# Attention, then two MLPs on one core: where 1 / sum is multiplied in, and when the weight product is made

## The chip, the cores and the metric

The kernel runs on one core of a Trainium2 chip. The metric is the device time of one execution in microseconds. The core has a tensor engine (TensorE, PE in the profile; PEld is its weight load), VectorE (DVE), ScalarE (ACT), GpSimd (POOL) and SyncE (SP), which here only issues transfers. Each engine works through its own list of instructions in order; semaphores make one wait for another.

## The reference

Attention with RMS-normed q and k over 4 batches of 12 heads, 448 positions and 64 features, and then two MLPs over the 1792 tokens of 768 features:

```python
def rmsnorm(x, g):
    return x / np.sqrt(np.mean(x * x, axis=-1, keepdims=True) + 1e-06) * g
scores = 1.0 / np.sqrt(D) * np.matmul(rmsnorm(q, g_q), rmsnorm(k, g_k).transpose(0, 1, 3, 2))
attn = np.exp(scores - np.max(scores, axis=-1, keepdims=True))
attn = attn / (np.sum(attn, axis=-1, keepdims=True) + 1e-09)
x = np.matmul(attn, v).transpose(0, 2, 1, 3).reshape(B * S, H * D)
h = x @ w_in                                  # 768 x 2048
x = np.maximum(0.01 * h, h) @ w_out           # 2048 x 768
return ((x @ w1) * (x @ w2) @ w3) @ w_out2    # 768 x 1024, 1024 x 1024, 1024 x 768
```

The MLP weights arrive as 64-bit floats.

## The kernel before, in words

The heads are worked off in 24 pairs `t`, each in two halves; a half is a *slot*, and slot `2t + half` holds the scores of pair `t`, chunks `2 half` and `2 half + 1` of 112 query rows. `attention_steps` writes the work of a slot in this order: at an even slot the value product of pair `t - 2` (`values`), then the four transposes of p for head `s - 2` (`p_transpose`), then `scores`; after an odd slot come the keys of the next pair (`keys`: transposes into `pk`, split into `kh` and `kl`), the load of q and the squares for the norm three pairs ahead (`statistics`); after an even slot the loads of v and of the rows of q and k three pairs ahead. `run_later` issues at the end of a slot the transfers that were put off.

`scores` multiplies in three passes (high and low parts of q and k, 12 matmuls a slot, tile `ps`), VectorE takes the scaled minimum out of PSUM into `p` (L254), ScalarE makes the exponent in place and sums it along the row (L263). Then VectorE makes `r = 1 / (sum + 1e-9)` for the half (L268, L269), and GpSimd multiplies each of the four `p` tiles by it, row by row (L272), before the tensor engine transposes them (L286). The value product `po` holds the two heads of a pair, 64 features each, over 128 partitions, with the 448 positions along the free axis. For batches 0 and 1 `split` makes of it the high part `xh` (ScalarE) and the low part `xl` (VectorE), both out of PSUM; for batches 2 and 3 ScalarE copies it to `x`, and SP stores that to `xd` in DRAM.

Between the attention's steps a generator of other work is drawn on, at a pace that `fill` sets from the slots that it is given. First `combine_weights` makes `wc = w3 x w_last` (tile `pw`, 384 matmuls); it stands in slots 5 to 17, by `COMBINE_SLOTS`. From there to slot 26 the first MLP of batch 0 runs for two of its four groups (the *early* part, tile `ps_mm`), then the *late* part with batch 1 and the rest; batches 2 and 3 follow as the *last pair* when the heads are done. The weights come as 64-bit words over ScalarE's queue (the first four over SP's); GpSimd, ScalarE and VectorE turn each tile into a float32 (`raw`, on VectorE L427 and L431) and split it into `wh` and `wl` (or `lasth` and `lastl` for w_last, on VectorE L184). The weights of the early part are kept in DRAM as high and low parts for the late one (`kept_first_mlp_h`, `_l`), which GpSimd's queue stores and SP's loads.

In which order the instructions of an engine stand is decided when the program is built, by a list scheduler that takes what is ready in its own model of time, by priority; `issue_after` ties an instruction behind another on its engine.

Of the kernel before, what the change touches and what calls it, by code (L numbers as in the profile page):

```python
# [8 lines left out]
F32 = mybir.dt.float32  # L9
# [3 lines left out]
ALU = mybir.AluOpType  # L13
# [23 lines left out]
KEYS_AHEAD = 1  # L37
P_TILES = 8
TOGETHER = 2000
COMBINE_SLOTS = 5, 17  # L40
EARLY = 2
PRIORITY = dict(
    values=200, p_transpose=600, scores=600, prep=600, load=100, statistics=100, keys=50
# [4 lines left out]
def attention_then_moe(  # L48
# [40 lines left out]
    def bank(name):  # L89
        return psum.tile([P, 512], F32, tag="ps", name=name)  # L90
# [45 lines left out]
    def statistics(t):  # L136

        if t >= NH // 2:
            return
        x = pairs[t]["rows"]  # L140
        ss = small.tile([CP, 2, 2, NCH], F32, tag="ss", name="ss", bufs=2)
        after = exps.get(t - STATS_AHEAD)
        for part in (1, 0):
            y = x[:, part]
            if part:
                y = io.tile([CP, 2, NCH, D], F32, tag="sq", name="sq", bufs=1)
            with tc.issue_after(after.ins) if after else ExitStack():
                nc.scalar.activation(y, x[:, part], AF.Square)
            nc.vector.tensor_reduce(ss[:, part], y, axis=AX.X, op=ALU.add)
        nc.vector.tensor_scalar(ss, ss, 1.0 / D, 1e-6, op0=ALU.mult, op1=ALU.add)  # L150
        rs = small.tile([CP, 2, 2, NCH], F32, tag="rs", name="rs", bufs=4)
        y = small.tile([CP, 2, 2, NCH], F32, tag="y", name="y", bufs=2)
        nc.scalar.activation(y, ss, AF.Ln)
        nc.scalar.activation(rs, y, AF.Exp, scale=-0.5)
        nc.vector.scalar_tensor_tensor(y, rs, -0.5, rs, op0=ALU.mult, op1=ALU.mult)  # L155
        nc.vector.tensor_tensor(y, y, ss, op=ALU.mult)
        nc.vector.scalar_tensor_tensor(rs, y, 1.5, rs, op0=ALU.add, op1=ALU.mult)
        nc.vector.tensor_scalar_mul(rs[:, 0], rs[:, 0], -1.0 / D**0.5)
        pairs[t]["scale"], pairs[t]["rk"] = rs[:, 0], rs[:, 1]
# [65 lines left out]
    def scores(t, half):  # L225

        if t >= NH // 2:
            return
        x = pairs[t]
        pair = heads[2 * t : 2 * t + 2]  # L230
        if half == 0:
            x["sums"] = small.tile([CP, 2, NCH], F32, tag="sum", name="sum")
            for h in pair:
                h["p"] = [None] * NCH
        ps = [[bank("ps")[:CP, :S] for _ in range(2)] for _ in range(2)]
        chunks = range(2 * half, 2 * half + 2)
        terms = [("qh", "kh"), ("ql", "kh"), ("qh", "kl")]
        x["scored"] = together(
            (
                ps[c % 2][e],  # L240
                x[q][mine(e), c * CP : (c + 1) * CP],
                x[k][mine(e)],
                n == 0,
                n == len(terms) - 1,
            )
            for c in chunks
            for n, (q, k) in enumerate(terms)
            for e in range(2)
        )
        for c in chunks:  # L250
            for e, h in enumerate(pair):
                p = h["p"][c] = att.tile([CP, S], F32, tag="p", name="p", bufs=P_TILES)
                low = small.tile([CP, 1], F32, tag="low", name="low", bufs=8)
                nc.vector.tensor_scalar(  # L254
                    p,
                    ps[c % 2][e],
                    x["scale"][:, e, c : c + 1],
                    None,
                    op0=ALU.mult,
                    op1=ALU.min,  # L260
                    accum_out=low,
                )
                exps[t] = nc.scalar.activation(  # L263
                    p, p, AF.Exp, bias=low, scale=-1.0, accum_out=x["sums"][:, e, c : c + 1]
                )

        r = small.tile([CP, 2, 2], F32, tag="r", name="r")
        nc.vector.tensor_scalar_add(r, x["sums"][:, :, 2 * half : 2 * half + 2], 1e-9)  # L268
        nc.vector.reciprocal(r, r)  # L269
        for c in chunks:  # L270
            for e, h in enumerate(pair):
                nc.gpsimd.tensor_scalar(  # L272
                    h["p"][c], h["p"][c], r[:, e, c % 2 : c % 2 + 1], 1.0, op0=ALU.mult, op1=ALU.mult
                )

    def mine(i):
        return slice(D * (i % 2), D * (i % 2 + 1))
# [20 lines left out]
    def split(x, hi, lo, eng="P"):  # L298

        copy("A", hi, x)  # L300
        subtract(eng, lo, x, hi)
# [6 lines left out]
    def values(t):  # L308
# [5 lines left out]
        if j == 0 and b < PB:  # L314
# [4 lines left out]
            for kc in reversed(range(NCH))  # L319
            for e in (1, 0)  # L320
        )
        if b < PB:
            split(po[:, :S], *(y[:, j // 2] for y in xt[b]), "V")
        else:
            x = att.tile([P, S], F32, tag="x", name="x", bufs=1)
            copy("A", x, po[:, :S])
            later.append(lambda: nc.sync.dma_start(xd[b - PB, j // 2], x))
        for h in (*pair, pairs[t]):
            h.clear()
# [8 lines left out]
    def ranked(f, *args):  # L338
        with tc.high_priority(PRIORITY.get(f.__name__, 0)):
            f(*args)  # L340

    def attention_steps():

        for t in range(NH // 2 + 2):
            ranked(values, t - 2)
            yield 2 * t
            for half in range(2):
                s = 2 * t + half
                for kc in range(NCH):
                    ranked(p_transpose, s - 2, kc)  # L350
                    yield s
                ranked(scores, t, half)
                for _ in range(NCH):
                    yield s
                if half:
# [721 lines left out]
```

## Time and profile before

| what | us |
|---|---|
| median of 3 runs (lowest, highest) | 1235.17 (1234.72, 1236.8) |
| the profiled execution | 1229.4 |
| its span, first to last instruction | 1227.6 |
| PE busy in it | 1157.6 (94%) |
| DVE busy | 777.9 (63%) |
| ACT busy | 662.7 (54%) |
| POOL busy | 390.2 (32%) |

Busy times are sums over the whole span; the stages in it have different limits, and an engine's idle time costs nothing where another sets the pace. The mean granted TensorE clock was 0.967 of full speed.

### The profile page before, as it was taken

The page shows a single profiled execution, that of the slowest core. Times are in us where ns is not written, and L with a number is a line of the kernel's source. Part 1 is how long each engine was busy: PE and PEld are TensorE (multiplying, and loading weights), DVE is VectorE, ACT ScalarE, POOL GpSimd, SP SyncE. Part 2 cuts the span into 40 slices and gives each one's busy share as a digit, 9 for nine tenths or more (in the row PEclk, how much of TensorE's full clock was granted, in tenths as well). Part 3 has the DMA queues.
Part 4 walks back from the last instruction along what each step waited for, and adds up shares of the span by engine and source line. Part 5 has one row for each costly group of instructions (what it writes and reads, how often), then busy time and mean ns, then how long its engine had stood idle before and what let it go on. Part 6 is the DMA issues. An engine that isn't in the chain of part 4 may idle for free.

```text
span 1227.6 us, 17006 instructions
## 1 busy us (share of the span) xinstructions
PE 1157.6 (94%) x6096; PEld 966.4 (79%) x6096; DVE 777.9 (63%) x1511; ACT 662.7 (54%) x1343; POOL 390.2 (32%) x474
## 2 busy tenths in 40 slices
PE   2779999998979999999999999999999999899998
PEld 1456778776668788888878888888999999699997
DVE  7997777889852375857854465276346455954553
ACT  7676667777644475666654664245443334533431
POOL 3654345677731344367642443200000000000000
PEclk8669999998889999999999999999999999999999
DMA  8433335877576534534421441062212021112202
GB/s 256 143 99 108 113 123 199 303 257 262 186 298 193 172 119 157 165 126 165 166 88 64 152 161 53 34 227 64 77 35 78 26 77 59 58 39 67 72 35 99
DMA packets 65381, 158.93 MB, mean 129 GB/s; under 512 B 7440, under 2 KB 32784, under 8 KB 65296
## 3 DMA queue, kind: packets, MB, share of 16 engines
q1 hardware_dynamic: 45648, 73.94, 19.0%
q10 hardware_dynamic: 10944, 49.29, 12.0%
q0 software_dynamic: 8704, 34.61, 7.5%
q8 instruction: 48, 0.79, 0.3%
q14 instruction: 37, 0.30, 0.1%
HBM read 114.95 MB, written 42.86 MB: 129 GB/s over the span
## 4 chain that ended last, share of the span: by engine, by line
PE 64%; DVE 7%; DMA 4%; ACT 1%; issue 1%; POOL 1%; SPq 0%; ACTq 0%; DVEq 0%; POOLq 0%
PE ps_mm L499 26%; PE ps_o L499 13%; PE ps_b L499 9%; PE ps_c L499 5%; PE po L123 3%; PE pt L286 3%; PE ps L123 3%; PE ps_a L499 2%; DVE ol L184 1%; DVE wl L184 1%; DMA wh<-kept_first_mlp_h 1%; DMA qk_sb<-qk 1%; DMA x_f<-xd 1%; DMA w<-w_out 1%; DVE acc L863 1%
## 5 line engine op out<-in xcount | busy, mean ns | idle before, releaser
L272 POOL TENSOR_SCALAR p<-p,r 112x448 f32<-112x448 f32 x192 | 150.9, 802 | 63.4 <-DVE r L269 34.4
L184 DVE TENSOR_TENSOR wl<-raw,wh 128x512 fp32r<-128x512 f32 (+1 forms) x136 | 113.9, 839 | 74.9 <-ACT wh L705 35.1
L499 PE MATMUL ps_mm<-xh,wh 128*128 128x448 f32 x384 | 143.0, 373 | 7.3 <-DMA wh<-kept_first_mlp_h 7.0
L263 ACT ACTIVATE p<-p,low 112x448 f32<-112x448 f32 x192 | 126.5, 661 | 40.4 <-DVE p L254 40.1
L499 PE MATMUL ps_mm<-xl,wh 128*128 128x448 f32 x384 | 146.8, 382 | 0.0
L499 PE MATMUL ps_mm<-xh,wl 128*128 128x448 f32 x384 | 141.9, 370 | 0.1
L254 DVE TENSOR_SCALAR_CACHE_REDUCE p<-ps,rs 112x448 f32<-112x448 f32 x192 | 122.0, 678 | 27.7 <-PE ps L123 27.7
L286 PE MATMUL pt<-ident,p 112*112 112x112 f32 x768 | 107.2, 278 | 25.7 <-POOL p L272 20.7
L286 PEld LDWEIGHTS pt<-ident,p 112*112 112x112 f32 x768 | 87.5, 143 | 52.8 <-POOL p L272 26.6
L499 PE MATMUL ps_mm<-gl,wh 128*128 128x448 f32 x288 | 109.5, 380 | 0.0
L427 DVE SCALAR_TENSOR_TENSOR raw<-w,raw 128x768 uint32<-128x768 uint32 (+1 forms) x80 | 76.0, 949 | 51.1 <-ACT w L425 50.9
L499 PE MATMUL ps_mm<-gh,wl 128*128 128x448 f32 x288 | 106.2, 369 | 0.9 <-DMA wl<-kept_first_mlp_l 0.9
L499 PE MATMUL ps_mm<-gh,wh 128*128 128x448 f32 x288 | 106.3, 372 | 0.6 <-DMA wh<-kept_first_mlp_h 0.6
L499 PE MATMUL ps_o<-gl,wh 128*128 128x448 f32 x288 | 104.1, 365 | 0.0
L499 PE MATMUL ps_o<-gh,wl 128*128 128x448 f32 x288 | 100.5, 365 | 0.0
L499 PE MATMUL ps_o<-gh,wh 128*128 128x448 f32 x288 | 99.1, 365 | 0.0
L420 POOL TENSOR_SCALAR raw<-w 128x768 f32<-128x768 f32 (+1 forms) x80 | 70.2, 878 | 84.3 <-DVE wl L184 51.9
L422 ACT ACTIVATE w<-w 128x768 uint32<-128x768 uint32 (+1 forms) x80 | 63.5, 794 | 47.0 <-DMA w<-w_out 16.1
L425 ACT ACTIVATE w<-w 128x768 f32<-128x768 f32 (+1 forms) x80 | 63.1, 789 | 45.6 <-POOL raw L420 45.6
L499 PEld LDWEIGHTS ps_mm<-xh,wh 128*128 128x128 f32 x384 | 73.0, 190 | 15.5 <-DVE y L155 6.3
L123 PE MATMUL po<-pth,v_sb 112*64 112x448 f32 x384 | 80.7, 562 | 1.9 <-ACT pth L101 1.1
L499 PEld LDWEIGHTS ps_mm<-xl,wh 128*128 128x128 f32 x384 | 73.2, 191 | 10.8 <-issue 4.9
(136 smaller groups left out, 2650.8 us busy)
## 6 DMA issues: line engine op xcount, KB each, us to landing
w<-w_in ACTq DMA_DIRECT2D x16, 768.0 KB, 4.8
w<-w_out ACTq DMA_DIRECT2D x24, 512.0 KB, 3.8
w<-w ACTq DMA_DIRECT2D x16, 768.0 KB, 4.5
qk_sb<-qk SPq DMA_DIRECT2D x48, 224.0 KB, 4.2
w<-w3t ACTq DMA_DIRECT2D x16, 512.0 KB, 3.3
kept_first_mlp<-raw POOLq DMA_DIRECT2D x16, 384.0 KB, 4.7
kept_first_mlp<-raw POOLq DMA_DIRECT2D x24, 256.0 KB, 3.5
kept_second_mlp<-raw POOLq DMA_DIRECT2D x16, 384.0 KB, 3.0
```

The source lines that it names most:

```text
L123: one = nc.tensor.matmul(out, a, x, start=begin, stop=end)
L184: e.tensor_tensor(out, x, y.bitcast(F32), op=ALU.subtract)
L254: nc.vector.tensor_scalar(p, ps[c % 2][e], x["scale"][:, e, c : c + 1], None, op0=ALU.mult, op1=ALU.min, accum_out=low,)
L263: exps[t] = nc.scalar.activation(p, p, AF.Exp, bias=low, scale=-1.0, accum_out=x["sums"][:, e, c : c + 1])
L272: nc.gpsimd.tensor_scalar(h["p"][c], h["p"][c], r[:, e, c % 2 : c % 2 + 1], 1.0, op0=ALU.mult, op1=ALU.mult)
L286: nc.tensor.transpose(pt[:, c * CP : (c + 1) * CP], h["p"][c][:, kc * CP : (kc + 1) * CP], ident[:CP, :CP],)
L420: nc.gpsimd.tensor_scalar(out, h, 0.0, 1.0, op0=ALU.mult, op1=ALU.mult)
L422: nc.scalar.activation(low, low, AF.Copy, scale=2.0**-29)
L425: nc.scalar.activation(h, h, AF.Copy, scale=2.0**-112)
L427: nc.vector.scalar_tensor_tensor(top, high, 3, top, op0=ALU.logical_shift_left, op1=ALU.bitwise_or)
L499: nc.tensor.matmul(ps[:, :n], a, x, start=begin, stop=end, skip_group_check=on)
L863: nc.vector.tensor_tensor(acc[m, b], ps[:, :S], acc[m, b], op=ALU.add)
```

## The change

Three things. First, `p` stays undivided: `scores` no longer scales it on GpSimd. `normalise`, which runs once a pair after its second half, makes `r` for all four chunks of both heads, and puts off two steps for SP: `store` writes `r` to a DRAM tensor `rd` as two rows of 448, and `spread`, one `run_later` on, loads each row into the 64 partitions of its head (`rb`, two buffers). `values` multiplies `po` out of PSUM by `rb` on VectorE, in place in `rb`; the split for batches 0 and 1 then reads that tile, with its subtraction on GpSimd, and for batches 2 and 3 SP stores it. Second, the squares of `statistics` go to a PSUM bank where they had a tile in SBUF. Third, `COMBINE_SLOTS` goes from 5, 17 to 1, 14.

```diff
--- before.py
+++ after.py
@@ -37,7 +37,7 @@
 KEYS_AHEAD = 1
 P_TILES = 8
 TOGETHER = 2000
-COMBINE_SLOTS = 5, 17
+COMBINE_SLOTS = 1, 14
 EARLY = 2
 PRIORITY = dict(
     values=200, p_transpose=600, scores=600, prep=600, load=100, statistics=100, keys=50
@@ -143,7 +143,7 @@
         for part in (1, 0):
             y = x[:, part]
             if part:
-                y = io.tile([CP, 2, NCH, D], F32, tag="sq", name="sq", bufs=1)
+                y = bank("sq")[:CP].rearrange("p (h c d) -> p h c d", h=2, c=NCH)
             with tc.issue_after(after.ins) if after else ExitStack():
                 nc.scalar.activation(y, x[:, part], AF.Square)
             nc.vector.tensor_reduce(ss[:, part], y, axis=AX.X, op=ALU.add)
@@ -264,14 +264,25 @@
                     p, p, AF.Exp, bias=low, scale=-1.0, accum_out=x["sums"][:, e, c : c + 1]
                 )
 
-        r = small.tile([CP, 2, 2], F32, tag="r", name="r")
-        nc.vector.tensor_scalar_add(r, x["sums"][:, :, 2 * half : 2 * half + 2], 1e-9)
+    def normalise(t):
+
+        if t >= NH // 2:
+            return
+        r = small.tile([CP, 2, NCH], F32, tag="r", name="r")
+        nc.vector.tensor_scalar_add(r, pairs[t]["sums"], 1e-9)
         nc.vector.reciprocal(r, r)
-        for c in chunks:
-            for e, h in enumerate(pair):
-                nc.gpsimd.tensor_scalar(
-                    h["p"][c], h["p"][c], r[:, e, c % 2 : c % 2 + 1], 1.0, op0=ALU.mult, op1=ALU.mult
-                )
+        rd = dram.tile([2, S], F32, name=f"rd{t}")
+        rb = pairs[t]["rb"] = io.tile([P, S], F32, tag="rb", name="rb", bufs=2)
+
+        def store():
+            nc.sync.dma_start(rd.rearrange("n (p c) -> p n c", c=NCH), r)
+            later.append(spread)
+
+        def spread():
+            for e in range(2):
+                nc.sync.dma_start(rb[mine(e)], rd[e : e + 1].to_broadcast([D, S]))
+
+        later.append(store)
 
     def mine(i):
         return slice(D * (i % 2), D * (i % 2 + 1))
@@ -319,11 +330,11 @@
             for kc in reversed(range(NCH))
             for e in (1, 0)
         )
+        x = pairs[t]["rb"]
+        nc.vector.tensor_tensor(x, po[:, :S], x, op=ALU.mult)
         if b < PB:
-            split(po[:, :S], *(y[:, j // 2] for y in xt[b]), "V")
+            split(x, *(y[:, j // 2] for y in xt[b]))
         else:
-            x = att.tile([P, S], F32, tag="x", name="x", bufs=1)
-            copy("A", x, po[:, :S])
             later.append(lambda: nc.sync.dma_start(xd[b - PB, j // 2], x))
         for h in (*pair, pairs[t]):
             h.clear()
@@ -350,6 +361,8 @@
                     ranked(p_transpose, s - 2, kc)
                     yield s
                 ranked(scores, t, half)
+                if half:
+                    ranked(normalise, t)
                 for _ in range(NCH):
                     yield s
                 if half:
```

The order of the instructions moves with it. On VectorE, at the start of the program, these rows stood from the low part of the first keys on (`w_665` and so on are the 64-bit tiles of w_last, `lastl` the low part of a finished one):

```order
L219 SCALAR_TENSOR_TENSOR kl<-pk,gqk,kh 128x448
L427 SCALAR_TENSOR_TENSOR raw<-w_665,raw 128x768
L254 TENSOR_SCALAR p,low<-ps,rs 112x448 x2
L431 ISA raw<-w_665,raw 128x1536
L427 SCALAR_TENSOR_TENSOR raw<-w_667,raw 128x768
L254 TENSOR_SCALAR p,low<-ps,rs 112x448 x2
L431 ISA raw<-w_667,raw 128x1536
L254 TENSOR_SCALAR p,low<-ps,rs 112x448
L184 TENSOR_TENSOR lastl<-raw,lasth 128x768
L254 TENSOR_SCALAR p,low<-ps,rs 112x448
```

and these stand there now, from soon after `kl` on to the first `p`:

```order
L184 TENSOR_TENSOR lastl<-raw,lasth 128x768
L444 ISA raw<-w_312,raw 128x1536
L204 TENSOR_TENSOR qk_sb<-qk_sb,rs 112x2x4x64
L158 TENSOR_SCALAR rs<-rs 112x8
L440 SCALAR_TENSOR_TENSOR raw<-w_314,raw 128x768
L184 TENSOR_TENSOR lastl<-raw,lasth 128x768
L444 ISA raw<-w_314,raw 128x1536
L440 SCALAR_TENSOR_TENSOR raw<-w_316,raw 128x768
L149 TENSOR_REDUCE ss<-sq 112x8
L149 TENSOR_REDUCE ss<-qk_sb 112x8
L444 ISA raw<-w_316,raw 128x1536
L184 TENSOR_TENSOR lastl<-raw,lasth 128x768
```

The conversions of the first four tiles of w_last, which stood between the first minima, now stand ahead of them. On the tensor engine the program before went through slots 0 to 6 with attention alone; these are the rows from the value product of pair 1, at the start of slot 6, up to the first matmul of the weight product:

```order
L123 MATMUL po<-pth,v_sb 64x448 x8
L286 MATMUL pt<-ident,p 112x112 x4
L123 MATMUL ps<-kh,qh 112x448 x2
L123 MATMUL ps<-kh,ql 112x448 x2
L123 MATMUL ps<-kl,qh 112x448 x2
L123 MATMUL ps<-kh,qh 112x448
L286 MATMUL pt<-ident,p 112x112 x4
L123 MATMUL ps<-kh,qh 112x448
L123 MATMUL ps<-kh,ql 112x448 x2
L123 MATMUL ps<-kl,qh 112x448 x2
L286 MATMUL pt<-ident,p 112x112 x24
L499 MATMUL pw<-lasth,wh 128x384
```

Now the first one follows the transposes of slot 2, ahead of the scores of slot 3; here from the keys of pair 1 on:

```order
L209 MATMUL pk<-ident,qk_sb 128x112 x4
L297 MATMUL pt<-ident,p 112x112 x12
L123 MATMUL ps<-kh,qh 112x448 x2
L123 MATMUL ps<-kh,ql 112x448 x2
L297 MATMUL pt<-ident,p 112x112 x4
L123 MATMUL ps<-kl,qh 112x448 x2
L123 MATMUL ps<-kh,qh 112x448 x2
L123 MATMUL ps<-kh,ql 112x448 x2
L123 MATMUL ps<-kl,qh 112x448 x2
L297 MATMUL pt<-ident,p 112x112 x16
L512 MATMUL pw<-lasth,wh 128x384
```

The weight product moved ahead by about two pairs. On SP, where the rows of q and k of pairs 6 to 8 are loaded, there stood

```order
L167 DMA qt_sb_1573<-qt 128x448
L178 DMA v_sb_1113<-v 112x2x256
L134 DMA qk_sb_859<-qk 112x2x256 x2
L134 DMA qk_sb_1119<-qk 112x2x256 x2
L167 DMA qt_sb_1890<-qt 128x448
L178 DMA v_sb_1424<-v 112x2x256
L167 DMA qt_sb_2192<-qt 128x448
L178 DMA v_sb_1743<-v 112x2x256
L134 DMA qk_sb_1430<-qk 112x2x256 x2
L167 DMA qt_sb_2625<-qt 128x448
```

and there stands now, up to the store of pair 4's r and the v behind it, with `rd` the stores of r and `rb` the loads into 64 partitions:

```order
L178 DMA v_sb_1017<-v 112x2x256
L167 DMA qt_sb_1761<-qt 128x448
L278 DMA rd3_1121<-r_1118 112x2x4
L134 DMA qk_sb_1023<-qk 112x2x256 x2
L283 DMA rb_812<-rd2_811 64x448 x2
L178 DMA v_sb_1324<-v 112x2x256
L134 DMA qk_sb_1330<-qk 112x2x256 x2
L283 DMA rb_1122<-rd3_1121 64x448 x2
L167 DMA qt_sb_2050<-qt 128x448
L278 DMA rd4_1426<-r_1423 112x2x4
L178 DMA v_sb_1612<-v 112x2x256
```

The two loads of a pair's `rb` stand behind the next loads of `qk`, and some behind the next pair's store.

## Rows read from the trace of the kernel before

**Rows 1.** Busy time of each engine by stretch: us, engines, clock, DMA share, GB/s.

```profile
14.60:57.90 43.30, 24.90 (x110) 14.70 (x110) 41.48 (x86) 36.08 (x74) 23.24 (x22) 0.68 0.55 178
57.90:103.80 45.90, 38.26 (x192) 25.76 (x191) 36.15 (x88) 30.23 (x71) 26.34 (x29) 0.74 0.33 103
103.80:234.10 130.30, 128.83 (x772) 100.72 (x771) 100.53 (x218) 89.04 (x201) 66.08 (x90) 1.00 0.51 169
234.10:398.70 164.60, 150.04 (x799) 114.89 (x798) 116.05 (x237) 103.60 (x227) 93.25 (x125) 0.93 0.68 242
398.70:828.00 429.30, 425.80 (x2352) 357.72 (x2352) 256.58 (x507) 239.56 (x486) 177.41 (x202) 1.00 0.39 132
828.00:1227.60 399.60, 388.79 (x1876) 351.91 (x1874) 219.75 (x363) 157.87 (x275) 0.00 (x0) 0.99 0.19 60
```

**Rows 2.** TensorE in order of time: start, us, instruction; slot marks and pw.

```profile
57.85 0.46 PE L123 MATMUL ps<-kh,qh 64*112 64x448 f32 x2
...
103.82 0.45 PE L123 MATMUL ps<-kh,qh 64*112 64x448 f32 x1
...
204.69 0.34 PE L499 MATMUL pw<-lasth,wh 128*128 128x384 f32 x1
...
209.38 0.33 PE L499 MATMUL pw<-lasth,wh 128*128 128x384 f32 x1
...
234.07 0.45 PE L123 MATMUL ps<-kh,qh 64*112 64x448 f32 x1
...
398.74 0.46 PE L123 MATMUL ps<-kh,qh 64*112 64x448 f32 x2
```

**Rows 3.** Chain of waits, unbroken TensorE pieces: start, us, what.

```profile
463.89 3.16 PE po L123 x16
...
531.23 7.41 PE ps_mm L499 x36
...
629.26 1.91 PE ps L123 x12
...
790.60 1.53 PE pt L286 x16
```

**Rows 4.** Waits of TensorE up to 398.7 us: total, times, longest.

```profile
PE pt L286 <- POOL p L272: 20.7, 8, 10.4
...
PE ps_mm L499 <- DMA wh<-kept_first_mlp_h: 7.0, 2, 6.1
```

**Rows 5.** Waits of SP's DMA queue up to 398.7 us.

```profile
SPq L134 <- PE pk L209: 162.3, 11, 31.4
```

**Rows 6.** Loads of qk up to 398.7 us, from issue to landing.

```profile
DMA to landing us min/median/max: 2.6/4.2/9.1
```

**Rows 7.** Groups by line and form up to 398.7 us: busy, mean ns, idle before.

```profile
L272 POOL TENSOR_SCALAR p<-p,r 112x448 f32<-112x448 f32 x112 | 89.6, 816 | 20.4 <-DVE r L269 11.1 <-PE ps_mm L499 3.1 <-PE ps L123 2.8
...
L184 POOL TENSOR_TENSOR ql<-qt_sb,qh 128x448 fp32r<-128x448 f32 x16 | 20.3, 1269 | 30.1 <-ACT qh L101 28.0 <-issue 2.0
...
L268 DVE TENSOR_SCALAR r<-sum 112x4 f32<-112x4 f32 x28 | 8.0, 284 | 9.8 <-ACT p L263 9.8
...
L184 DVE TENSOR_TENSOR xl<-po,xh 128x448 fp32r<-128x448 f32 x12 | 7.4, 618 | 4.7 <-ACT xh L101 4.6
...
L156 DVE TENSOR_TENSOR y<-y,ss 112x16 f32<-112x16 f32 x17 | 4.9, 286 | 0.3
```

**Rows 8.** One line up to 398.7 us: ns min/median/max, first and last start.

```profile
L156 DVE TENSOR_TENSOR y<-y,ss x17: 140/174/1148, 11.6 to 395.3; 112x16 f32<-112x16 f32 x17
```

**Rows 9.** VectorE in order of time at the first p.

```profile
17.18 0.67 DVE L254 TENSOR_SCALAR_CACHE_REDUCE p<-ps,rs 112x448 f32<-112x448 f32 x1
...
18.39 0.94 DVE L431 CUSTOM_DVE_ANT_0 raw<-w,raw 128x1536 uint16<-128x1536 uint16 x1
...
19.26 0.94 DVE L427 SCALAR_TENSOR_TENSOR raw<-w,raw 128x768 uint32<-128x768 uint32 x1
```

## The prediction

> **What bounds the kernel now.** I read the busy times by stretch first, then the order and the prices of the tensor work, then the waits. The tensor engine's share of the whole span is an average over stages with different limits, so I cut the span at the first score matmul of slots 0, 4, 8, 18 and 28, which stand at 14.6, 57.9, 103.8, 234.1 and 398.7 us [rows 1, 2]. From slot 28 on the tensor engine is busy 425.8 of 429.3 us and then 388.8 of 399.6, with the clock granted at its higher level, 2.4 GHz, for all but a hundredth [rows 1]: nothing there can get faster unless matmuls go away, and none do. All that can be won lies before 398.7 us.
>
> There I count what the tensor engine must do at full clock. The prices come from unbroken pieces of the chain of waits [rows 3]: 36 ps_mm in 7.41 us (0.206 each), 16 pt in 1.53 (0.096; I take the same for a pk, which is a transpose too), 12 ps in 1.91 (0.159), 16 po in 3.16 (8 in the program, 0.395 each); and pw 0.174, from 27 starts between 204.69 and 209.38 [rows 2]. Counted in the program order up to the marks, for before:
> - to slot 4: 12 pk, 48 ps, 36 pt, 8 po, no pw: 15.4 us of work in 57.9, so 42.5 us beyond it;
> - slots 4 to 8: 27.0 us of work (31 pw in it) in 45.9, 18.9 beyond;
> - slots 8 to 18: 121.0 in 130.3, 9.3 beyond;
> - slots 18 to 28: 137.6 in 164.6, 27.0 beyond.
> Together 97.7 us. The second and fourth figure can be read a second way from the windows [rows 1]: idle plus the share by which the granted clock falls short, the time at 1.2 GHz counting half. In slots 4 to 8 that is 7.6 idle plus 0.26 x 45.9 = 11.9; in slots 18 to 28 it is 14.6 plus 0.07 x 164.6 = 11.5.
>
> Who is waited for: up to slot 4 VectorE is busy 41.5 of 43.3 us [rows 1] and the engines behind it starve; the longest list of tensor waits up to 398.7 is "pt waits for POOL p", 20.7 us in 8 waits, 10.4 of it one wait [rows 4]. Between slots 4 and 8 no engine is full; the tensor engine is granted 0.74 of its clock in the mean. At the end of the fourth stretch it waits 6.1 us for a kept weight [rows 4].
>
> **The change part by part.** *The scaling of p on GpSimd goes.* 112 instructions of 816 ns, 89.6 us up to slot 28, leave POOL [rows 7], which is busy 209 us from slot 0 to slot 28 [rows 1]. The transposes then start when the exponent is done.
>
> *r is made once a pair.* Up to slot 28 there are 28 adds of 284 ns [rows 7] and as many reciprocals; half of them go: 4 us of VectorE for the adds, and 2 to 4 for the reciprocals, bounded by the price of a small instruction in its shortest form, 0.14 us [rows 8], and by the adds.
>
> *The multiply.* The value product is multiplied on VectorE out of PSUM instead of being subtracted from; the nearest row is that subtraction, xl<-po,xh, one operand from PSUM and one from SBUF, 618 ns [rows 7]: 12 for 12 in the first two batches, and 12 more later, where VectorE is busy 257 of 429 us [rows 1]. The low half goes to POOL, 12 instructions of 1.3 us by the nearest row, ql<-qt_sb,qh [rows 7], against 90 us freed. Squares go to PSUM: one more bank for the time from square to sum; the same reduction out of PSUM I take at its 0.68 us, since reading 448 elements from PSUM (two p in 1.21 us [rows 9]) shows no surcharge. Bounds: 0 and, if a bank is missing, one matmul group's wait of about 2 us a pair in slots 4 to 28, 24 us.
>
> *The trip through DRAM.* Per pair one store of 224 pieces of 16 bytes and two loads, all on SP. The store has two slots of cover. The loads stand behind the next qk loads, and these wait for pk: SP waited 162.3 us for that [rows 5]. So rb is issued about 1.6 us after pk (two issues of qk and two of rb at some 0.4 us) and lands 2.6 to 9.1 us later, 4.2 in the middle, by the qk loads [rows 6]. In VectorE's order the multiply stands behind kl of the same pk with 4 to 7 us of work between. Middle case: 5.8 us against about 6.5, no wait. Upper bound: 10.7 against 6.5, 4 us a pair. Queued behind a waiting multiply are the p minima and pth copies of the same slot, and the tensor engine waits for these. I take 0; where it goes wrong is rival B.
>
> *The weight product from slot 1.* Its 384 matmuls are 66.7 us of filler. In the new order, 25 of them stand before slot 4, 121 before slot 8, all before slot 14. The work ahead of the marks is then 20.9, 58.3, 176.9 and again 301.0 us at slot 28: from there both programs have the same number of each kind ahead, so the time of slot 28's first scores decides.
> The price: in VectorE's order ten more conversion instructions and one more pair of reductions stand before the first p. At 0.87 us for a conversion [rows 9] and 0.6 for a reduction that is 9.9 us. Before, these conversions ran between the p; so slot 0 starts some 10 us later, and slot 4 also, as VectorE has no gap there; four r instructions less and fewer stalls give back some 1.5.
>
> **The sum**, as tensor work plus what lies beyond it:
> - to slot 4: 20.9 of work, mark at 57.9 + 8.5 = 66.4, so 45.5 beyond (bounds 42.5 less 5.5 of filler, no delay at all, so 37, and 52: the delay and as much as one qk landing of 6 us on top);
> - slots 4 to 8: 37.4 of work. With 90 pw to fill in, idle and half clock should halve: 8 beyond (bounds 2, and 18.9 as before);
> - slots 8 to 18: 118.6, and 9 beyond, as before (6 to 12);
> - slots 18 to 28: 124.1. VectorE loses 10 us of work there (the early MLP's conversions are spread over 12 slots instead of 9) and POOL a third. I take half of 27: 14 (bounds 5, and 27 as before).
> Beyond: 76.5 against 97.7, a gain of 21 us. All lower bounds give 50, a gain of 48; all upper ones 110, a loss of 12. The profiled execution took 1229.4 us with a span of 1227.6; the median of the runs is 1235.2. Taken from the median: **1214 us**.
>
> One rule of the Trainium skill is weighed here. First the row: y<-y,ss on VectorE, 16 elements, has a median of 174 ns and a maximum of 1148 [rows 8], with a mean of 286 [rows 7]: 0.11 us a piece are lost. Some 250 instructions that are as small or read two operands from SBUF stand up to slot 28; at the same loss they come to an estimated 28 us. The Trainium skill, SBUF — State Buffer, section "Who interferes with whom", says that VectorE and GpSimd share one pair of ports as an exclusive lock, so that an instruction of one can stand still until one of the other has ended; the trace agrees as far as single rows go, since 1148 ns is 174 plus about one POOL instruction. By that rule the freed 89.6 of 209 us of POOL would hand back 43% of the 28, 12 us of VectorE, and the sum would be 1202; without it, 1214.
>
> **The rivals.** *A, as summed:* 1214, its own range 1203 to 1226. Chance 0.55.
>
> *B, slower: the multiply waits for rb.* Place: the multiply in VectorE's queue, slots 4 to 28, 12 pairs. With rb landing 9.1 us after issue each loses 4 us, 48 in all; half of it reaching the tensor engine is 24 and the late weights behind the same SP queue some 7 more: 1245. It decides from a landing of about 8 us on, where 12 pairs lose 3 us and eat the gain with what hangs behind. For it: landing times up to 9.1 and an in-order queue that now holds three more transfers a pair. Against: the median of 4.2. Chance 0.13.
>
> *C, nearly nothing: the filler helps only on paper.* If VectorE keeps setting the pace to slot 8 and the fourth stretch stays as before, beyond is 45.5 + 15 + 9 + 24 = 93.5: 1231. For it: VectorE's total work hardly falls. Chance 0.15.
>
> *D, more: VectorE also gets its stalls back* (43% of 28 us, 12) and 2 of the 6.1 us of the late wait go: 1200. For it: the maximum of y<-y,ss, six times its median [rows 8]. Against: POOL also issues the kept weights' stores, which stay. Chance 0.17.
>
> **How the numbers follow.** The predicted time is A's. What a measurement of this kernel tells from no change is about 0.2%, 2.5 us. Faster: A, D and some 6 of C's 15 hundredths, 0.78. Same: 0.06 from C. Slower: B and the rest of C, 0.16. The range reaches from D's 1200 less a little to just past C and the start of B, 1199 to 1237; A's own range is 1203 to 1226.
>
> **What would show it.** Right: pw matmuls from about 41 us on, in slot 3 instead of slot 7 (the first p at 17.2 + 9.9, and some 14 us of VectorE's rows up to the first low part of w3); slot 4 at 64 to 69 us, slot 8 at 107 to 115, slot 28 at 370 to 385; full clock from slot 8 on at the latest; no "pt waits for POOL p"; the stretch from slot 28 to the end within 3 us of 829. Wrong: VectorE idle ahead of the multiply with a DMA of rb as the releaser, over 2 us a pair; SP stuck on rd stores with kept weights behind it; slot 4 later than 72 us; or a tensor engine that still runs at 0.7 of its clock between slots 4 and 8.

## The result, and the profile after

The changed kernel takes 1223.75 us in the median of 4 runs (1221.2 to 1227.45), the kernel before 1235.38 beside it: a ratio of 0.9907, 95% interval 0.9883 to 0.9931, or 11.6 us less. The forecast was 1214 and a gain of 21. The profiled execution took 1223.49 with a span of 1221.7; the one of before lay 6 us under its own median, so the two spans differ by only 5.9.

Busy time by stretch of the changed kernel, cut at the starts of slots 0, 4, 8, 18, 28 and at 820 us; columns as in [rows 1]:

```profile
13.85:63.68 49.83, 30.72 (x146) 20.83 (x146) 47.54 (x96) 43.37 (x87) 17.06 (x14) 1.00 0.66 204
63.68:114.11 50.43, 46.52 (x249) 34.61 (x249) 38.65 (x91) 33.51 (x79) 12.96 (x14) 0.87 0.39 119
114.11:243.85 129.74, 126.56 (x746) 96.10 (x745) 98.36 (x206) 91.20 (x204) 51.68 (x67) 1.00 0.62 202
243.85:388.40 144.55, 134.83 (x731) 100.60 (x732) 97.46 (x213) 91.53 (x204) 52.66 (x69) 0.96 0.74 242
388.40:820.00 431.60, 428.52 (x2358) 360.42 (x2358) 256.97 (x497) 235.69 (x476) 114.45 (x122) 1.00 0.43 137
820.00:1221.70 401.70, 388.89 (x1870) 352.19 (x1868) 220.40 (x364) 157.75 (x275) 0.00 (x0) 0.99 0.20 61
```

Minus the tensor work of the prediction (20.9, 37.4, 118.6, 124.1), the first four stretches hold 42.8, 13.0, 11.1 and 20.5 us beyond it, 87.4 together, where before had 97.7 and the forecast 76.5. GpSimd's load in the fourth stretch is 52.7 us against 93.3 [rows 1].

What TensorE waits for up to slot 28 (us, times, longest):

```profile
PE ps L123 <- DVE ss L149: 12.2, 4, 8.5
PE pk L209 <- DVE qk_sb L204: 12.1, 1, 12.1
PE ps L123 <- DVE rb L334: 4.2, 3, 1.8
```

"pt waits for GpSimd's p", 20.7 us before [rows 4], is gone. At the head of the list stands a new wait: the scores wait for VectorE's reduction ss, since that reads the squares out of the PSUM bank which the scores want. The pk wait is the start of the program and was there before. Then VectorE's wait for rb, the landing of the transfers that read or write rb over the whole span (48 loads, 12 stores of x), VectorE's first p, its 1024-wide conversion, and the small instruction of [rows 8]:

```profile
DVE rb L334 <- DMA rb<-rd: 1.6, 1, 1.6
...
DMA to landing us min/median/max: 1.9/5.0/10.2
...
28.63 0.67 DVE L254 TENSOR_SCALAR_CACHE_REDUCE p<-ps,rs 112x448 f32<-112x448 f32 x1
...
L444 DVE CUSTOM_DVE_ANT_0 raw<-w,raw 128x1024 uint16<-128x1024 uint16 x28 | 20.7, 741 | 0.3
...
L156 DVE TENSOR_TENSOR y<-y,ss x17: 159/174/1114, 10.0 to 384.7; 112x16 f32<-112x16 f32 x17
```

The multiply waited for rb once, 1.6 us. The first p comes at 28.63, against 17.18 [rows 9].

### The profile page after: what moved, and what is told of

Its sections match the earlier page's. It is cut to its first block, busy times and chain, and to the rows that moved or that the text cites. A ratio compares the mean times of both kernels' runs of the same rounds, so it can differ in the third digit from the quotient of the medians.

```text
span 1221.7 us, 16781 instructions
## 1 busy us (share of the span) xinstructions
PE 1157.0 (95%) x6096; PEld 965.4 (79%) x6096; DVE 765.1 (63%) x1475; ACT 658.6 (54%) x1331; POOL 252.6 (21%) x294
## 4 chain that ended last, share of the span: by engine, by line
PE 65%; DVE 9%; DMA 6%; ACT 3%; issue 2%; POOL 0%; SPq 0%; ACTq 0%; DVEq 0%; POOLq 0%
PE ps_mm L512 27%; PE ps_o L512 13%; PE ps_b L512 9%; PE ps_c L512 5%; PE pt L297 3%; PE po L123 3%; PE ps L123 3%; PE ps_a L512 2%; DMA w<-w_out 2%; DMA qk_sb<-qk 1%; DVE ol L184 1%; DMA x_f<-xd 1%; DVE wl L184 1%; DVE raw L444 1%; DVE raw L440 1%
## 5 line engine op out<-in xcount | busy, mean ns | idle before, releaser
L184 DVE TENSOR_TENSOR wl<-raw,wh 128x512 fp32r<-128x512 f32 (+1 forms) x136 | 111.2, 820 | 84.9 <-ACT wh L469 44.6
L254 DVE TENSOR_SCALAR_CACHE_REDUCE p<-ps,rs 112x448 f32<-112x448 f32 x192 | 121.7, 679 | 30.6 <-PE ps L123 30.6
L297 PEld LDWEIGHTS pt<-ident,p 112*112 112x112 f32 x768 | 83.5, 138 | 33.3 <-issue 7.0
L297 PE MATMUL pt<-ident,p 112*112 112x112 f32 x768 | 99.7, 271 | 8.9 <-ACT p L263 3.7
L440 DVE SCALAR_TENSOR_TENSOR raw<-w,raw 128x768 uint32<-128x768 uint32 (+1 forms) x80 | 69.9, 874 | 43.1 <-ACT w L438 43.0
L469 ACT ACTIVATE wh<-raw 128x512 fp32r<-128x512 f32 (+1 forms) x84 | 59.2, 705 | 42.3 <-PE ps_mm L512 37.4
L123 PE MATMUL ps<-kh,qh 64*112 64x448 f32 x192 | 61.0, 448 | 21.3 <-DVE ss L149 12.2
L512 PEld LDWEIGHTS ps_mm<-xh,wl 128*128 128x128 f32 x384 | 72.6, 189 | 7.4 <-issue 1.9
```

What stands on the lines that cost most here:

```text
L123: one = nc.tensor.matmul(out, a, x, start=begin, stop=end)
L184: e.tensor_tensor(out, x, y.bitcast(F32), op=ALU.subtract)
L254: nc.vector.tensor_scalar(p, ps[c % 2][e], x["scale"][:, e, c : c + 1], None, op0=ALU.mult, op1=ALU.min, accum_out=low,)
L297: nc.tensor.transpose(pt[:, c * CP : (c + 1) * CP], h["p"][c][:, kc * CP : (kc + 1) * CP], ident[:CP, :CP],)
L440: nc.vector.scalar_tensor_tensor(top, high, 3, top, op0=ALU.logical_shift_left, op1=ALU.bitwise_or)
L469: self.rounded = nc.scalar.activation(flat[0], x, AF.Copy)
```

## The experiments

Each kernel was timed in five rounds against the kernel before. Squares in SBUF are float32 in e2, e6, e7 and e8, as in the kernel before, and bfloat16 in e1, e5 and e9 to e12; VectorE's sum of them takes 681 ns in the mean as float32 (e8) and 682 as bfloat16 (e11). The order of the instructions is made anew for each kernel, so more moves than the lines of an edit. The tensor work up to slot 28 is 301.0 us in all of them, so the start of slot 28 less 301.0 is again the time beyond it. The ratios come from all executions, the slot columns from one profiled execution each: before's lay 6 us under the median, e11's 7 us and e4's 4 us above it.

| kernel | slots | scaling | squares | ratio (95%) | slot 8 | slot 28 | beyond |
|---|---|---|---|---|---|---|---|
| before | 5, 17 | GpSimd | SBUF | 1 | 103.8 | 398.7 | 97.7 |
| e6 | 1, 17 | GpSimd | SBUF | 0.9966 (0.9950–0.9982) | 107.5 | 396.4 | 95.4 |
| e7 | 5, 14 | GpSimd | SBUF | 0.9929 (0.9912–0.9946) | 102.5 | 391.9 | 90.9 |
| e2 | 1, 14 | GpSimd | SBUF | 0.9904 (0.9882–0.9926) | 112.3 | 386.6 | 85.6 |
| e4 | 5, 17 | GpSimd | PSUM | 1.0022 (1.0008–1.0036) | 110.4 | 404.9 | 103.9 |
| e5 | 5, 17 | trip | SBUF | 0.9928 (0.9905–0.9952) | 100.8 | 390.5 | 89.5 |
| e3 | 5, 17 | trip | PSUM | 1.0026 (1.0002–1.0050) | 103.2 | 403.4 | 102.4 |
| e1 | 1, 14 | trip | SBUF | 0.9891 (0.9868–0.9913) | 105.2 | 384.3 | 83.3 |
| after | 1, 14 | trip | PSUM | 0.9907 (0.9883–0.9931) | 114.1 | 388.4 | 87.4 |
| e8 | 1, 14 | none | SBUF | 0.9722 (0.9702–0.9743) | 100.0 | 367.5 | 66.5 |
| e9 | 1, 14 | trip, no multiply | SBUF | 0.9880 (0.9852–0.9908) | 104.4 | 380.4 | 79.4 |
| e10 | 1, 14 | multiply, no trip | SBUF | 0.9717 (0.9691–0.9743) | 101.0 | 368.2 | 67.2 |
| e11 | 1, 14 | GpSimd's load alone | SBUF | 0.9878 (0.9852–0.9905) | 104.7 | 387.4 | 86.4 |
| e12 | 1, 14 | trip, issued by GpSimd | SBUF | 0.9804 (0.9775–0.9834) | 105.7 | 379.7 | 78.6 |

**e1: squares out of PSUM.**

```diff
-                y = bank("sq")[:CP].rearrange("p (h c d) -> p h c d", h=2, c=NCH)
+                y = io.tile([CP, 2, NCH, D], mybir.dt.bfloat16, tag="sq", name="sq", bufs=1)
```

> The changed kernel with the squares of the statistics back in SBUF, as a bfloat16 tile (float32 does not fit there), so that no PSUM bank holds them; their sums are rougher by that. The gain was 11.6 us where I summed 21, and I had costed the squares' bank at nothing with an upper bound of 24. Theory T1, the bank is the missing part: the 12.2 us in which scores wait for VectorE's reduction (4 waits, 8.5 of it at 26 us) go, slot 4 comes 3 to 8 us earlier than 63.7 us, and the kernel takes 1215 to 1220 us against 1223.75. Rival R2, the bank is harmless, because VectorE sets the pace at the start and the scores would only have waited for something else: within 2.5 us of 1223.75, and the same time goes to another releaser.

1220.0 us, 0.9891. The first p is back at 16.2 us and the ps wait for ss is gone; counted by this kernel's own order (35.5 us of tensor work in slots 4 to 8, 121.7 in 8 to 18), slots 4 to 8 fall from 13.0 to 8.3 us beyond it, and 8 to 18 rise from 11.1 to 12.1. The time is at the edge of T1's range, but slot 4 came only 2.4 us earlier, not 3 to 8. The ratio is 0.16% under that of the whole change, 2 us, and the two intervals overlap: with the new slots the bank's price is not resolved, between T1 and R2.

**e2: the slots alone.**

```diff
 (the kernel before)
-COMBINE_SLOTS = 5, 17
+COMBINE_SLOTS = 1, 14
```

> The kernel before with the weight product alone moved from slots 5 and 17 to slots 1 and 14; p is still scaled on GpSimd, squares in SBUF. Theory T1, the two parts need each other: with GpSimd still scaling p the conversions and the scaling crowd the first slots, the filler helps about half, 1227 to 1232 us. Rival R1, the slots make all of the gain: 1221 to 1225. Rival R3, the filler is worth nothing by itself, the delay of the first p eats it: 1234 or more.

0.9904, 1222.0 us: rival R1. The slots alone give as much as the whole change, while GpSimd still scales p and TensorE still waits for it 23.0 us. T1 falls.

**e3: the change without the slots.**

```diff
 (the changed kernel)
-COMBINE_SLOTS = 1, 14
+COMBINE_SLOTS = 5, 17
```

> The changed kernel with the weight product back in slots 5 and 17; the normalising through DRAM and the squares in PSUM stay. Theory T1: the waits for GpSimd's p go (20.7 us before slot 28, of which the tensor engine gets perhaps a third back where VectorE sets the pace), the squares' bank costs some of it: 1228 to 1233 us. Rival R1, all of the gain comes from the slots: 1234 to 1238. Rival R4, all of it comes from the normalising: 1222 to 1226.

1238.4 us, 1.0026: without the slots the change costs 3 us. T1 and R4 fall, and R1 is missed by 0.4 us at its slow end. TensorE's waits of this kernel show what came in for the pt waits:

```profile
PE ps L123 <- DVE ss L149: 15.8, 5, 9.5
...
PE ps L123 <- DVE rb L334: 7.3, 7, 2.0
```

**e4: the squares' bank alone.**

```diff
 (the kernel before)
-                y = io.tile([CP, 2, NCH, D], F32, tag="sq", name="sq", bufs=1)
+                y = bank("sq")[:CP].rearrange("p (h c d) -> p h c d", h=2, c=NCH)
```

> The kernel before with the squares alone moved to PSUM. Theory T1, the bank costs tensor waits: scores or transposes wait for VectorE's reductions for 6 to 12 us in slots 0 to 28, and the kernel takes 1238 to 1243 us against 1235.4. Rival R2, harmless: within 2.5 us of 1235.4.

1236.6 us, 1.0022, 2.7 us by the ratio: a cost whose interval lies above 1, but in R2's range, although the scores waited 12.3 us for ss. In e3, e4 and after, seven or eight conversions of the weight product, two or three low parts and a third pair of reductions stand in VectorE's order ahead of the first p (at 28.0, 28.2 and 28.6 us), whatever the slots; in the kernel before, e1 and e2 a single conversion does (17.2, 16.2 and 16.2 us).

**e5: the normalising alone.** e1 with slots 5 and 17.

> The kernel before with the normalising through DRAM alone: weight product in slots 5 and 17, squares in SBUF (as bfloat16, sums rougher). Theory T2, after four runs: the slots make the gain (0.9904 with them alone, 0.9907 with the whole change), the normalising is worth nothing, because the tensor engine's wait for GpSimd's p stood in time that VectorE sets anyway. T2 expects a ratio of 0.998 to 1.002 to the kernel before. Rival R5, the normalising is worth a gain that the squares' bank hides in the third run (1.0026): 0.992 to 0.997. Rival R6, it costs (trip through DRAM, waiting multiply): 1.003 or more.

0.9928: T2 falls, R5 holds. The trip in place of GpSimd's scaling gives 9 us with the old slots, and the squares' bank eats all of it there (0.9928 to 1.0026, 12 us; the intervals lie apart). With the new slots the normalising adds next to nothing (0.9904 to 0.9891).

**e6 and e7: one end of the weight product at a time.**

```diff
 (the kernel before)
-COMBINE_SLOTS = 5, 17
+COMBINE_SLOTS = 1, 17        e7: 5, 14
```

> The kernel before with the weight product from slot 1 to slot 17: an earlier start alone, so that the filler is thinner in each slot and the early MLP still starts where it did. With the slots alone at 1 and 14 the time beyond tensor work fell by 7.5 us up to slot 8, rose by 3 in slots 8 to 18, fell by 7.8 in slots 18 to 28. Theory T2, both ends count, each in its own stretch: a ratio of 0.994 to 0.997. Rival R7, the start makes all of it: 0.989 to 0.992. Rival R8, the end makes all of it: 0.999 or more.

> The kernel before with the weight product from slot 5 to slot 14: an earlier end alone, so that the early MLP starts three slots sooner and is spread over twelve slots in place of nine. Theory T2: 0.993 to 0.997, from slots 18 to 28. Rival R7, the start makes all of it: 0.999 or more. Rival R8, the end makes all of it: 0.989 to 0.992.

0.9966 and 0.9929: the earlier start gives 0.34%, the earlier end 0.71%, and their sum, 1.05%, is e2's 0.96% within the intervals. Both ends count, as T2 said, the end by a hair more than its range. The first of the two expectations counts e2 with the changed kernel's tensor work; by e2's own order its time beyond tensor work fell by 5.8 us up to slot 8, rose by 0.6 in slots 8 to 18 and fell by 7.1 in slots 18 to 28.

**e8: no normalising.** e2 without r and without the scaling on GpSimd, nothing in their place.

> The kernel before with slots 1 and 14 and with the normalising left out of the computation: no sums' reciprocal, no scaling on GpSimd, nothing in its place, so it bounds from above what any way of normalising can give. Theory T2, GpSimd's scaling was covered: within 0.003 of the slots alone, 0.987 to 0.993. Rival R9, taking the scaling out is worth 8 us or more, and the trip through DRAM with its multiply gives it back: 0.978 to 0.985.

0.9722, beyond both ranges: 22 us under e2 and 21 under e1. So there was much to win by taking the scaling off GpSimd, and something in the new way of normalising costs as much. The next three kernels look for both.

**e9: the trip without the multiply** (slots up to 28).

```diff
 (e1)
-        nc.vector.tensor_tensor(x, po[:, :S], x, op=ALU.mult)
         if b < PB:
-            split(x, *(y[:, j // 2] for y in xt[b]))
+            split(po[:, :S], *(y[:, j // 2] for y in xt[b]), "V")
         else:
+            nc.vector.tensor_tensor(x, po[:, :S], x, op=ALU.mult)
```

> The changed kernel with squares in SBUF (bfloat16), with r and its trip through DRAM as they are, but rb not multiplied in up to slot 28: the low half is subtracted from PSUM on VectorE, as in the kernel before, so the first two batches are not divided by their sums. With no normalising at all and the same slots the ratio was 0.9722, with the changed normalising 0.9891: 21 us that I had summed as near nothing. Theory T3, VectorE's busy time sets the mark of slot 28 (340.6 us busy and a mark of 398.7 in the kernel before; 330.5 and 384.3; 316.1 and 367.5 with no normalising): this kernel keeps r on VectorE and has a subtraction for each multiply, so 0.986 to 0.991. Rival R10, the multiply with its wait for rb is the price: 0.974 to 0.981.

0.9880, in T3's range: the multiply with its wait for rb costs nothing that can be told from e1. A subtraction stands on VectorE for each multiply, so this prices the wait and not VectorE's work; e10 prices that. (The busy times in the expectation are larger than those by stretch, which are 301.6, 291.8 and 277.7 us up to slot 28; their differences are nearly the same.)

**e10: the multiply without the trip.** rb is filled with ones.

```diff
 (e1)
-        rd = dram.tile([2, S], F32, name=f"rd{t}")
...
-        def store():
-            nc.sync.dma_start(rd.rearrange("n (p c) -> p n c", c=NCH), r)
-            later.append(spread)
...
-        later.append(store)
+        nc.gpsimd.memset(rb, 1.0)
```

> The same kernel with the multiply in place but without the trip through DRAM: r is made and thrown away, and rb is filled with ones by GpSimd, so no probability is divided. Theory T3: VectorE's work is the same, so 0.986 to 0.991. Rival R11, the three transfers a pair on SP's queue are the price, since they hold up what stands behind them (a kept weight's wait of 4.5 us, kh waits of 9 us): 0.974 to 0.981.

0.9717, as fast as no normalising at all and a little past R11's range. T3 falls, and R11 names the part: the three transfers a pair are the price, 1.7% or 21 us, with the squares in SBUF. This run does not say by which route. r and the multiply, 9 us more of VectorE's busy time up to slot 28 (286.4 against e8's 277.7), cost nothing beside it.

**e11: GpSimd's load without its result.**

```diff
 (e8, squares in SBUF as bfloat16)
+        for c in chunks:
+            for e in range(2):
+                nc.gpsimd.tensor_scalar(
+                    idle, idle, x["sums"][:, e, c : c + 1], 1.0, op0=ALU.mult, op1=ALU.mult
+                )
...
+        nc.gpsimd.memset(idle, 0.0)
```

> The kernel with slots 1 and 14 and no normalising (0.9722), squares as bfloat16, with 112 instructions of the old scaling's shape and size put back on GpSimd before slot 28, but on a tile of zeros that nobody reads: each still waits for its sums, no transpose waits for it, and VectorE makes no r. Probabilities are not divided. The same slots with the real scaling gave 0.9904. Theory T3, GpSimd's work as such costs VectorE time (raw<-w,raw took 89.1 us with the scaling and 79.0 without, wl<-raw,wh 30.7 and 28.4), and r costs the rest: 0.979 to 0.985. Rival R12, the price is the transposes' wait for GpSimd's p (23.0 us before slot 28) and GpSimd's load alone is harmless: 0.970 to 0.975. Rival R13, GpSimd's load is the whole price: 0.988 to 0.992.

0.9878, R13: 112 instructions on a tile that nobody reads cost 19 us, nearly all that the real scaling costs. Busy times up to slot 28, and VectorE's two 512- and 1024-wide conversions (busy, mean ns), in e8:

```profile
0.00:367.50 367.50, 328.92 (x1873) 248.25 (x1873) 277.70 (x586) 262.14 (x583) 128.15 (x160) 0.94 0.63 212
...
L422 DVE CUSTOM_DVE_ANT_0 raw<-w,raw 128x1024 uint16<-128x1024 uint16 x28 | 21.2, 757 | 0.2
...
L418 DVE SCALAR_TENSOR_TENSOR raw<-w,raw 128x512 uint32<-128x512 uint32 x28 | 19.4, 694 | 13.8 <-ACT w L416 13.8
```

and in e11:

```profile
0.00:387.40 387.40, 337.93 (x1873) 253.33 (x1873) 296.93 (x586) 264.17 (x583) 227.35 (x273) 0.93 0.60 201
...
L429 DVE CUSTOM_DVE_ANT_0 raw<-w,raw 128x1024 uint16<-128x1024 uint16 x28 | 24.4, 870 | 0.2
...
L425 DVE SCALAR_TENSOR_TENSOR raw<-w,raw 128x512 uint32<-128x512 uint32 x28 | 24.0, 857 | 10.5 <-ACT w L423 10.5
```

VectorE executes the same 586 instructions and is busy 19.2 us longer, and slot 28 starts 19.9 us later, in an execution that lay 7 us above e11's median. The Trainium skill, SBUF — State Buffer, section "Who interferes with whom", has VectorE and GpSimd share one pair of ports as an exclusive lock; in particular an instruction with two inputs from SBUF contends with a GpSimd instruction that reads SBUF. The traces agree, instruction by instruction. A 1024-wide conversion that overlaps no arithmetic instruction of GpSimd takes 683 ns in the mean in e11 (8 of 28) and 685 in e8 (22 of 28); one that overlaps such an instruction takes 945 in e11 (20) and 1024 in e8 (6). Two of e11, with GpSimd's dummy instructions beside the first:

```profile
207.68 0.63 POOL L270 TENSOR_SCALAR idle<-idle,sum 112x448 f32<-112x448 f32 x1
207.81 3.96 DVE L425 SCALAR_TENSOR_TENSOR raw<-w,raw 128x512 uint32<-128x512 uint32 x1
211.20 1.08 POOL L270 TENSOR_SCALAR idle<-idle,sum 112x448 f32<-112x448 f32 x1
...
226.39 0.68 DVE L429 CUSTOM_DVE_ANT_0 raw<-w,raw 128x1024 uint16<-128x1024 uint16 x1
```

p and pth, which read PSUM, have 677 and 615 ns in the mean in both kernels. So GpSimd's load lengthens VectorE's instructions. That this length sets the time is not shown: in e10 the 1024-wide conversions take 862 ns in the mean, nearly e11's 870, and e10 is 20 us faster. GpSimd's other work also stands in its queue behind the 112, which waited 42.9 us for ScalarE's sums.

**e12: the trip issued by GpSimd.** The version that the runs pointed to, with the whole computation.

```diff
 (e1)
-            nc.sync.dma_start(rd.rearrange("n (p c) -> p n c", c=NCH), r)
+            nc.gpsimd.dma_start(rd.rearrange("n (p c) -> p n c", c=NCH), r)
...
-                nc.sync.dma_start(rb[mine(e)], rd[e : e + 1].to_broadcast([D, S]))
+                nc.gpsimd.dma_start(rb[mine(e)], rd[e : e + 1].to_broadcast([D, S]))
```

> The changed kernel with squares in SBUF (bfloat16) and the whole computation, but with the store of r and the two loads of rb issued by GpSimd in place of SP. The trip costs 1.7% (0.9891 with it, 0.9717 without). Theory T4, the price is SP's order: a store that waits for r holds up the loads of qk, qt and v behind it (SP stood 49.6 us on it up to slot 28, 28.3 us at once), and slots 14 to 20 lose 11 of the 16 us; with GpSimd, which has time, the ratio is 0.972 to 0.979, the best version so far. Rival R14, the transfers themselves (224 pieces of 16 bytes and two broadcasts a pair) slow the loads beside them, whoever issues them: 0.986 to 0.991. Rival R15, GpSimd's own queue pays (kept weights and low halves behind a store that waits for r): 0.982 to 0.995, with GpSimd's waits for r or for rd in the trace.

1210.1 us, 0.9804: the fastest version with the whole computation, 0.9% (11 us) under e1 with squares, slots and multiply the same, and still 0.9% over e10. That is between the ranges of T4 and R15: T4 had the direction and too much of the size. SP's queue in e1 from 175 us on (start, us, what):

```profile
174.77 0.32 SPq L278 DMA_DIRECT2D rd<-r  x1
175.20 0.39 SPq L178 DMA_DIRECT2D v_sb<-v  x1
210.18 0.31 SPq L278 DMA_DIRECT2D rd<-r  x1
210.58 0.41 SPq L178 DMA_DIRECT2D v_sb<-v  x1
211.08 0.41 SPq L167 DMA_DIRECT2D qt_sb<-qt  x1
211.58 0.88 SPq L134 DMA_DIRECT2D qk_sb<-qk  x2
```

and its sum of waits, with ScalarE's waits for the qk loads behind it, up to slot 28 of e1:

```profile
SPq L278 <- DVE r L273: 49.6, 11, 28.3
...
ACT sq L148 <- DMA qk_sb<-qk: 23.0, 9, 6.5
```

The same stretch of SP's queue in e10:

```profile
202.04 0.35 SPq L167 DMA_DIRECT2D qt_sb<-qt  x1
202.49 0.38 SPq L178 DMA_DIRECT2D v_sb<-v  x1
203.86 0.81 SPq L134 DMA_DIRECT2D qk_sb<-qk  x2
```

and ScalarE's wait there:

```profile
ACT sq L148 <- DMA qk_sb<-qk: 13.0, 9, 3.4
```

In e1 SP stood 28.3 us, up to 210.2, on a store whose r was not yet made, and v, qt and qk went out in one burst behind it, qk 7.7 us later than in e10, while slot 14 had started only 4.6 us later (188.4 against 183.8). Slots 14 to 20 then take 79.3 us in e1 and 68.3 in e10. The 28.3 us by themselves are not lost: at the same place SP stood in e10 as long, on GpSimd's ql, which frees the buffer for q:

```profile
SPq L167 <- POOL ql L184: 150.4, 14, 32.4
```

What differs is when the loads behind go out. The qk loads leave 23.1, 21.1 and 20.5 us after the starts of slots 14, 16 and 18 in e1, 20.0, 16.6 and 14.8 in e10, and 19.2, 20.2 and 15.7 in e12. In e1 the chain of waits runs there from r over SP's issues and the load to the squares:

```profile
207.85 2.07 DVE r L272
...
210.18 0.31 SPq L278
...
211.58 4.97 DMA qk_sb<-qk
216.57 0.64 ACT sq L148
```

That e12 gets 11 us back shows that the issuer counts; that SP's order is the whole of it is argued from these rows, and one speaks against it: ScalarE's wait for the qk loads is still 19.5 us in e12. With GpSimd as issuer that wait is on an engine with time to spare. What it stood on ahead of the stores and of the rb loads, up to slot 28 of e12 (us, times):

```profile
  DVE r L273: 13.3, 8
...
  DMA rd<-r: 11.7, 5
```

The 0.9% that stay are not settled. Slot 28 of e12 starts 11.4 us later than e10's; 4.2 of that is there at slot 4, and 4.3 comes between slots 16 and 18. For the transfers themselves speaks that the w_in loads land after 7.1 us in the median against 4.6 in e10 (12 each); for GpSimd's queue speak the waits above; for its hold on VectorE, that VectorE is busy 294.0 us up to slot 28 against 286.4. No run tells these apart.

## Why the prediction was right in direction and short in size

Faster was right, and 1223.75 lies inside the range of 1199 to 1237 and inside A's own, at its slow end. That it does is in part luck: two terms of some 20 us that the sum did not have nearly cancel. Point by point:

- **Up to slot 4**: 45.5 beyond forecast, 42.8 measured; the mark at 63.7 lies just below the 64 to 69 given. The 9.9 us of conversions ahead of the first p are there (28.63 against 27.1 forecast), but not because of the slots, as I had argued: e1 and e2 have the new slots and their first p at 16.2, e3 and e4 the old slots and their first p at 28. The squares' bank orders it so. The slots alone move slot 4 by 2.1 us (e2: 60.0).
- **Slots 4 to 8**: 8 forecast, 13.0 measured, mark 114.1 inside 107 to 115. The term that was mis-sized is the squares' bank, costed at 0 with a bound of 24: without it this stretch measures 8.3 (e1). Over the whole kernel it measured 2.7 us with everything else as before (e4), 12 with the trip and the old slots (e3 to e5), and about 2, unresolved, here.
- **Slots 8 to 28**: 9 and 14 forecast, 11.1 and 20.5 measured; slot 28 came at 388.4, outside the 370 to 385 given. The relief that was to make the 14 came, and more: VectorE lost 18.6 us of work in slots 18 to 28 where 10 were forecast, GpSimd 44% where it was a third. The earlier end of the weight product did what was said (e7: 0.9929), and the late wait for the kept weight fell from 7.0 us to 0.6. But **the step of the sum that failed is the trip through DRAM, taken at 0**. I had looked for its price at the multiply (rival B) and found cover there; the cover was real, 1.6 us of wait, and e9 shows the multiply free. Measured with squares in SBUF the trip costs 21 us (e1 to e10), and about half of that goes when GpSimd issues it (e12). The likely route is SP: each store stands in an in-order queue until r is made, and the loads of qk, qt and v stand behind it. I had counted only the place of the rb loads in that queue ("no wait. Upper bound ... 4 us a pair") and named "SP stuck on rd stores" among the signs of being wrong without a price. In the changed kernel itself this route shows little: SP waited 30.6 us for r in 12 waits, 6.8 the longest, the qk loads left 14.2 to 14.4 us after the starts of slots 14, 16 and 18, and 13.1 of the 20.2 us by which it reaches slot 28 later than e10 are there at slot 8. No run takes the trip out with the squares left in PSUM, so how these 20 us divide between trip and bank there is open.
- **GpSimd's scaling** was counted with no gain of its own but the waits, and D gave 12 us to VectorE's stalls with a chance of 0.17. Measured, GpSimd's load is worth 19 us (e8 to e11), more than D's; the transposes' wait for it, on which the eye falls first [rows 4], and r with it are worth about 3 (e11 to e2, intervals overlapping). What D said of VectorE came: up to slot 28 its instructions took 33.7 us more before, and 21.9 more now, than the medians of the same forms while GpSimd does no arithmetic, 11.8 us less against D's 12. D's time did not come. D's argument went by a row that does not show it, though: L156 stays at a median of 174 and a maximum of 1114 with the scaling gone, while the wide conversions fell (1024: 894 to 741 ns, groups by form up to slot 28).
- **After slot 28**: 829 within 3 us was forecast, and 833.3 measured, 4.4 more than before. The other kernels have 828 to 836 there in single profiles, so this is no cost of the change that I can name.
- **C**, filler only on paper, gave 1231; e2 shows the filler to be worth 12 us by itself.
- **The other signs**: the first pw came at 47.4 us, where 41 was forecast (e1, with its first p at 16.2, has it at 41.0); the granted clock rose from 0.74 to 0.87 in slots 4 to 8, and was 1.00 and then 0.96 up to slot 28, where full clock was forecast; the transposes' wait for GpSimd is gone, as forecast.

So the sum came out short not by one size but by two large terms of opposite sign that I had both near zero, GpSimd's load (19 us back) and the trip (21 us out), over a filler term (12 us) that I had about right in sum with the rest: 1235 less 12 (slots) less 22 (no scaling) gives e8's 1200; r and the multiply 0, the trip 21, the bank about 2, and 1224 is what was measured. These are steps along one path of kernels and no fixed prices: the slots are worth 12 us with GpSimd's scaling and 5 on top of the trip (e5 to e1), and the trip in place of the scaling is worth 9 with the old slots and next to nothing with the new.

## What to carry to other kernels

A transfer that waits for a result can cost less where its data is used (1.6 us of wait here) than in the queue where it is issued: ask what stands behind it there, and try it on an engine that has time (11 us here). A wait at the head of the list can be worth little (23 us of "pt waits for p", some 3 in the time, not resolved) while the engine named in it costs more by its mere load (19 us); a dummy load without readers tells the two apart, and leaving the whole part out bounds what any rewrite can give. Prices measured in one variant (squares in SBUF) need not be those of another. When two parts of a change give no more than one of them, look for a third that takes back.

## What was not expected of the hardware

The same 586 VectorE instructions took 19.2 us more (277.7 to 296.9) when GpSimd ran 112 more instructions of its own, with the 512-wide two-operand conversion going from 694 to 857 ns in the mean; beside no arithmetic of GpSimd it took 685 and 686. A store of 3.5 KB in 224 pieces landed after 4.1 us in the median of the twelve between 60 and 385 us of e1, while SP had stood 49.6 us in 11 waits for what these stores carry up to slot 28.
